# Scores of two heads in one slot, with the low parts of the queries on the two row halves of the array

## The chip, the core and the metric

The kernel runs on one core of one Trainium2 chip. The metric is the time of one execution on the device in microseconds (us); the number shown for a kernel is the median of its runs. TensorE does the matmuls and transposes and writes PSUM, VectorE (DVE) and ScalarE (ACT) do everything elementwise, GpSimd (POOL) little, SyncE (SP) issues most DMAs.

## The reference

Attention over 4 batches of 12 heads, 448 positions, 64 elements per head, then two feed-forward layers over all 1792 tokens, all in float32:

```python
q_n, k_n = rmsnorm(q, g_q), rmsnorm(k, g_k)
scores = (1 / sqrt(64)) * q_n @ k_n.T
attn = exp(scores - max(scores)); attn = attn / (sum(attn) + 1e-9)
x = (attn @ v), heads side by side -> (1792, 768)
x = (sigmoid(x @ w_gate) * (x @ w_val)) @ w_out      # d_ff 1536
out = relu(x @ w_in) ** 2 @ w_out2                   # d_ff 2048
```

## The kernel before

**Sweeps and slots.** The work goes batch by batch. Sweep `s` does both feed-forward layers of batch `s` in 68 steps; a step takes one block of weights and issues its matmuls (18 of 448 columns, line 526 to 528, in most steps; 18 or 24 of 384 columns, line 735 to 737, in the last 16). The attention of batch `s + 1` is laid between these steps: `slots_of` lists its pieces in slots, and after step `i` of the sweep as many slots are run as bring the count to `(i + 1) * total // 66`. A function given to `later(n, ...)` runs `n` steps on, and what is put in `mid` runs when the next step has taken its block. A planner then orders each engine's instructions at build time: it goes by program order as priority, takes an instruction when by its own timeline the inputs are there and the output's tile is free, and takes the next one of lower priority otherwise. Weights are split into high and low parts (`w_split`, lines 177 and 178) three blocks ahead.

**Number formats.** A float32 value is kept as a high part in fp32r, the rounded format that TensorE takes in one pass, and a low part, the rest. A product is then high by high, high by low and low by high. The layers' matmuls do this with three matmuls each.

**Attention of batches 2 and 3** (batches 0 and 1 use other functions, among them `s_mm`, line 275, with plain fp32 operands). Heads go in pairs, with head 0 on partitions 0 to 63 and head 1 on 64 to 127; queries go in four chunks of 112, two chunks (`c2`) at a time.

- `a_hi`, `a_lo`, `a_dma` make the operands of the scores. `ks[:, e]` has for head `e` the high part of the keys on the head's own 64 partitions and the low part on the other 64. `qs[:, e, z]` has the high (`z = 0`) or low (`z = 1`) part of the queries, copied by a DMA to the other 64 partitions too. A matmul over 128 rows so gives the product of a query part with both key parts at once.
- `s_mm2` (line 414): scores of one head and two chunks, four matmuls over 128 rows: both query parts against both key parts. Its tile is one of the pool `att`, which has two tiles of two PSUM banks.
- `s_max2`, `s_exp2`, `s_norm2`: maximum (line 421), exponential (line 433), division by the sum.
- `c_mm2` (lines 455, 456): transposes the weights of attention into an `att` tile; `c_hi` (lines 465, 468) copies the high part out on ScalarE and `c_lo` (lines 473, 477) the low part on VectorE, one step later.
- `pv_mm2` (lines 486, 488): seven matmuls with the values; `pv_half` (line 492) and `pv_add` (line 498) add the two halves of its output.

Slots before take one head each: scores of chunks 0 and 1, transposes of the last head's chunks 2 and 3, scores of chunks 2 and 3, values of the last head, transposes of chunks 0 and 1.

Of the kernel before, what the change touches and what calls it, by code (L numbers as in the profile page):

```python
# [8 lines left out]
F32 = mybir.dt.float32  # L9
# [8 lines left out]
def attention_moe_moe2_kernel(  # L18
# [57 lines left out]
    def att_tile():  # L76
        return att_p.tile([128, 2, 512], F32, tag="att", name="att")
# [325 lines left out]
    def a_dma(st):  # L403
        qs = st["qs"]
        for h in range(2):
            a = slice(h * D, (h + 1) * D)
            z = slice((1 - h) * D, (2 - h) * D)
            nc.sync.dma_start(out=qs[z, h].bitcast(F32), in_=qs[a, h].bitcast(F32))

    def s_mm2(st, e, c2, ps):  # L410
        for i in range(2):
            c = 2 * c2 + i
            for z in range(2):
                nc.tensor.matmul(  # L414
                    out=ps[:QR, i, :S], lhsT=st["qs"][:, e, z, c * QR:(c + 1) * QR], rhs=st["ks"][:, e],
                    start=(z == 0), stop=(z == 1))
        st["s", e, c2] = ps

    def s_max2(st, e, c2):
        nm = sm_p.tile([QR, 2], F32, tag="nm", name="nm")  # L420
        nc.vector.tensor_reduce(out=nm, in_=st["s", e, c2][:QR, :, :S], axis=AX.X, op=ALU.max, negate=True)  # L421
        rq = st["ms"][:, 1].rearrange("p (c h) -> p c h", h=2)[:, 2 * c2:2 * c2 + 2, e]
        with tc.high_priority(offset=200):
            nc.vector.tensor_tensor(out=nm, in0=nm, in1=rq, op=ALU.mult)  # L424
        st["nm", e, c2] = nm
# [23 lines left out]
    def c_mm2(st, e, c2):  # L449
        ps = att_tile().rearrange("p a (k c) -> p (a k) c", k=2)  # L450
        p = st.pop(("p", e, c2))
        for i in range(2):
            for kc in range(NF):
                k0 = i * (S + TAIL) + kc * 128
                nc.tensor.transpose(ps[:, kc, i * QR:(i + 1) * QR], p[:, k0:k0 + 128], ident[:QR, :QR])  # L455
        nc.tensor.transpose(ps[:, NF, 0:QR], p[:, NM:NM + 2 * TAIL], ident[:QR, :QR])
        if c2 == 0:
            parts = one.tile([128, NS, S], F32R, tag="pt", name="parts")
            st["ph", e], st["pl", e] = parts[:, 0:NF + 1], parts[:, NF + 1:NS]
        st["c", e, c2] = ps  # L460

    def c_hi(st, e, c2):
        ps, ph = st["c", e, c2], st["ph", e]
        cs = slice(c2 * QW, (c2 + 1) * QW)
        nc.scalar.copy(out=ph[:, 0:NF, cs], in_=ps[:, 0:NF, 0:QW])
        for i in range(2):
            a, c0 = slice(i * TAIL, (i + 1) * TAIL), c2 * QW + i * QR
            nc.scalar.copy(out=ph[a, NF, c0:c0 + QR], in_=ps[a, NF, 0:QR])

    def c_lo(st, e, c2):  # L470
        ps, ph, pl = st.pop(("c", e, c2)), st["ph", e], st["pl", e]
        cs = slice(c2 * QW, (c2 + 1) * QW)
        nc.vector.tensor_tensor(
            out=pl[:, :, cs], in0=ps[:, 0:NF, 0:QW], in1=ph[:, 0:NF, cs].bitcast(F32), op=ALU.subtract)
        for i in range(2):
            a, c0 = slice(i * TAIL, (i + 1) * TAIL), c2 * QW + i * QR
            nc.vector.tensor_tensor(
                out=ph[(1 - i) * TAIL:(2 - i) * TAIL, NF, c0:c0 + QR], in0=ps[a, NF, 0:QR],
                in1=ph[a, NF, c0:c0 + QR].bitcast(F32), op=ALU.subtract)

    def pv_mm2(st, e):
        o = st["o", e] = att_tile()[:, 0, :S]
        ph, pl = st.pop(("ph", e)), st.pop(("pl", e))
        for kc in range(NF + 1):
            lhsT = st["vs"][:, kc, 2 * e:2 * e + 2].rearrange("p a d -> p (a d)")
            nc.tensor.matmul(out=o, lhsT=lhsT, rhs=ph[:, kc], start=(kc == 0), stop=(kc == NF))  # L486
            if kc < NF:
                nc.tensor.matmul(out=o, lhsT=lhsT, rhs=pl[:, kc], start=False, stop=False)

    def pv_half(st, e):  # L490
        xt = st["xt"] = tmp_p.tile([128, 512], F32, tag="tmp", name="xt")
        nc.scalar.copy(out=xt[e * D:(e + 1) * D, :S], in_=st["o", e][(1 - e) * D:(2 - e) * D])

    def pv_add(st, e):
        a = slice(e * D, (e + 1) * D)
        if e == 0:
            st["o"] = one.tile([128, S], F32, tag="x32", name="x32")
        nc.vector.tensor_tensor(out=st["o"][a], in0=st.pop(("o", e))[a], in1=st.pop("xt")[a, :S], op=ALU.add)

    xtile, xplain = {}, {}  # L500

# [6 lines left out]
    mid = []  # L508

    def later(n, fn, *args):  # L510
        due.setdefault(now[0] + n, []).append((fn, args))
# [241 lines left out]
    def nxt(b, hp):  # L753
        return (b, hp + 1) if hp + 1 < HP else (b + 1, 0)
# [3 lines left out]
    def slots_of(b):  # L758
# [49 lines left out]
            mid.append((a_lo, (st,)))  # L808
            later(1, a_dma, st)

        def do_s2(key, e, c2):
            st = pairs[key]
            s_mm2(st, e, c2, att_tile())
            s_max2(st, e, c2)
            mid.append((s_exp2, (st, e, c2)))
            later(1, s_norm2, st, e, c2)

        def do_c2(key, e, c2):
            st = pairs[key]
            c_mm2(st, e, c2)  # L820
            c_hi(st, e, c2)
            later(1, c_lo, st, e, c2)

        def do_pv2(key, e):
            st = pairs[key]
            pv_mm2(st, e)
            pv_half(st, e)
            later(1, pv_add, st, e)
            if e == 1:
                later(2, x_hi, st)  # L830
                later(2, x_lo, st)
                later(2, lambda: pairs.pop(key))

        def do_stat(key):
            st = pairs[key]
# [5 lines left out]
                later(2, stat_hat, st, 1)  # L841

        if b > 1:
            for h in range(H):
                key, e = (b, h // 2), h % 2
                nk = nxt(*key)
                prev = ((b, (h - 1) // 2), (h - 1) % 2)
                more = nk[0] < B

                def some(fn, nk=nk, more=more):  # L850
                    return [lambda: fn(nk)] if more else []

                add(lambda key=key, e=e: do_s2(key, e, 0), *(some(do_load) if e == 0 else []))
                if h:
                    add(lambda prev=prev: do_c2(*prev, 1))
                add(lambda key=key, e=e: do_s2(key, e, 1))
                if e == 1 and more:
                    add(*some(do_a2))
                if h:
                    add(lambda prev=prev: do_pv2(*prev))  # L860
                if e == 0:
                    add(lambda key=key: do_c2(key, 0, 0), lambda key=key: split_v(pairs[key]), *some(do_stat))
                else:
                    add(lambda key=key: do_c2(key, 1, 0), *some(do_v))
            add(lambda: do_c2((b, HP - 1), 1, 1))
            add(lambda: None)
            add(lambda: do_pv2((b, HP - 1), 1))
            return slots
        if b == 1:
            add(lambda: do_stat((1, 0)))  # L870
# [199 lines left out]
```

## Time and profile before

| what | value |
|---|---|
| median of 3 runs | 1279.74 us (1278.72 to 1280.75) |
| the profiled execution's own time | 1279.0 us |
| its span, first to last instruction | 1277.2 us |
| granted TensorE clock, mean | 0.999 of 2.4 GHz |
| TensorE busy | 1263.8 us, 99% of the span |
| VectorE busy | 941.3 us, 74% |
| ScalarE busy | 798.7 us, 63% |

A busy TensorE is one that has at least one matmul in flight; records of successive matmuls overlap, since they are pipelined, so the spacing from start to start tells what one costs. The chain of work that ended last lies on TensorE for 94% of the span.

### The profile page before, as it was taken

The page shows a single profiled execution, that of the slowest core. Times are in us where ns is not written, and L with a number is a line of the kernel's source. Part 1 is how long each engine was busy: PE and PEld are TensorE (multiplying, and loading weights), DVE is VectorE, ACT ScalarE, POOL GpSimd, SP SyncE. Part 2 cuts the span into 40 slices and gives each one's busy share as a digit, 9 for nine tenths or more (in the row PEclk, how much of TensorE's full clock was granted, in tenths as well). Part 3 has the DMA queues.
Part 4 walks back from the last instruction along what each step waited for, and adds up shares of the span by engine and source line. Part 5 has one row for each costly group of instructions (what it writes and reads, how often), then busy time and mean ns, then how long its engine had stood idle before and what let it go on. Part 6 is the DMA issues. An engine that isn't in the chain of part 4 may idle for free.

```text
span 1277.2 us, 19296 instructions
## 1 busy us (share of the span) xinstructions
PE 1263.8 (99%) x6755; PEld 1111.9 (87%) x6755; DVE 941.3 (74%) x1657; ACT 798.7 (63%) x1582; POOL 154.8 (12%) x152
## 2 busy tenths in 40 slices
PE   8999999999999999999999999999999999999998
PEld 6545888878878999999999999999999999999998
DVE  6857888788974888778876488877897546646964
ACT  5757887667865777656755477765666455524552
POOL 3301422212120001000100000100010001110000
PEclk9999999999999999999999999999999999999999
DMA  5445899897786344344344433433333456663364
GB/s 144 120 133 157 292 333 301 255 298 237 243 289 179 94 111 129 96 119 121 96 104 133 123 106 105 126 102 113 97 92 108 129 183 218 217 220 108 112 185 149
DMA packets 163616, 206.92 MB, mean 162 GB/s; under 512 B 77248, under 2 KB 123840, under 8 KB 163520
## 3 DMA queue, kind: packets, MB, share of 16 engines
q1 hardware_dynamic: 154176, 172.20, 46.6%
q0 software_dynamic: 7488, 33.04, 6.5%
q8 instruction: 53, 0.87, 0.3%
q10 hardware_dynamic: 1856, 0.46, 0.2%
q14 instruction: 43, 0.35, 0.1%
HBM read 161.61 MB, written 38.54 MB: 157 GB/s over the span
## 4 chain that ended last, share of the span: by engine, by line
PE 94%; DVE 2%; ACT 1%; DMA 1%; issue 1%; SPq 1%; POOL 0%; DVEq 0%; ACTq 0%; POOLq 0%
PE acc L526 19%; PE acc L528 19%; PE acc L527 19%; PE acc L737 4%; PE acc L735 4%; PE acc L736 4%; PE att L414 3%; PE att L275 3%; PE att L455 2%; PE acc L329 2%; PE att L486 2%; PE acc L606 2%; PE acc L608 2%; PE acc L607 2%; PE att L329 1%; PE acc L647 1%
## 5 line engine op out<-in xcount | busy, mean ns | idle before, releaser
L526 PE MATMUL acc<-xy,wsp 128*128 128x448 f32 x936 | 345.8, 370 | 2.0 <-ACT wsp L177 1.4
L178 DVE TENSOR_TENSOR wsp<-wraw,wsp 128x768 fp32r<-128x768 f32 x280 | 268.2, 958 | 106.8 <-ACT wsp L177 103.5
L528 PE MATMUL acc<-xy,wsp 128*128 128x448 f32 x936 | 344.5, 368 | 1.5 <-DVE wsp L178 1.5
L527 PE MATMUL acc<-xy,wsp 128*128 128x448 f32 x936 | 344.1, 368 | 0.1
L177 ACT CAST wsp<-wraw 128x768 fp32r<-128x768 f32 x280 | 233.4, 834 | 116.1 <-PE acc L528 38.8
L526 PEld LDWEIGHTS acc<-xy,wsp 128*128 128x128 f32 x936 | 176.3, 188 | 23.4 <-ACT wsp L177 4.3
L528 PEld LDWEIGHTS acc<-xy,wsp 128*128 128x128 f32 x936 | 176.3, 188 | 19.0 <-DVE wsp L178 2.1
L527 PEld LDWEIGHTS acc<-xy,wsp 128*128 128x128 f32 x936 | 176.3, 188 | 15.0 <-issue 0.7
L245 POOL TENSOR_TENSOR ms<-ms,mhalf 112x16 f32<-112x16 f32 (+1 forms) x25 | 84.5, 3381 | 546.8 <-DVE ms L244 456.4
L526 PE MATMUL acc<-hb,wsp 128*128 128x448 f32 x288 | 106.1, 369 | 0.0
L527 PE MATMUL acc<-hb,wsp 128*128 128x448 f32 x288 | 105.8, 367 | 0.0
L528 PE MATMUL acc<-hb,wsp 128*128 128x448 f32 x288 | 105.6, 367 | 0.0
L433 ACT ACTIVATE p<-att,nm,ms 112x448 f32<-112x448 f32 x96 | 68.8, 723 | 45.1 <-DVE nm L424 44.9
L736 PE MATMUL acc<-wsp,rb 128*128 128x384 f32 x288 | 96.9, 337 | 0.0
L737 PE MATMUL acc<-wsp,rb 128*128 128x384 f32 x288 | 96.8, 336 | 0.0
L735 PE MATMUL acc<-wsp,rb 128*128 128x384 f32 x288 | 96.4, 336 | 0.0
L151 ACT ACTIVATE wraw<-raw 128x768 f32<-128x768 f32 x64 | 58.4, 914 | 31.5 <-DVE wsp L178 19.2
L293 ACT ACTIVATE p<-att,nm 112x448 f32<-112x448 f32 x88 | 55.2, 635 | 15.4 <-DVE nm L281 13.8
L421 DVE TENSOR_REDUCE nm<-att 112x2 f32<-112x896 f32 x48 | 52.3, 1089 | 13.0 <-PE att L414 11.9
L159 DVE SCALAR_TENSOR_TENSOR wraw<-wraw,raw 128x768 int32<-128x768 int32 x64 | 61.0, 956 | 0.9
L166 POOL DMA_DIRECT2D w<-wraw x64 | 36.1, 564 | 206.5 <-DVE wraw L159 196.3
L527 PEld LDWEIGHTS acc<-hb,wsp 128*128 128x128 f32 x288 | 54.1, 188 | 5.7 <-DVE wraw L159 0.7
(169 smaller groups left out, 2209.3 us busy)
## 6 DMA issues: line engine op xcount, KB each, us to landing
wraw<-w SPq DMA_DIRECT2D x188, 384.0 KB, 3.1
w<-wraw POOLq DMA_DIRECT2D x64, 384.0 KB, 6.1
raw<-in_moe_w_out_dram SPq DMA_DIRECT2D x28, 768.0 KB, 7.8
raw<-in_moe_w_in_dram SPq DMA_DIRECT2D x16, 768.0 KB, 6.1
raw<-in_moe_w_gate_dram SPq DMA_DIRECT2D x12, 768.0 KB, 6.1
raw<-in_moe_w_val_dram SPq DMA_DIRECT2D x12, 768.0 KB, 6.3
wsrc<-w SPq DMA_DIRECT2D x16, 384.0 KB, 4.3
wt<-wdst POOLq DMA_DIRECT2D x32, 192.0 KB, 2.4
```

Source lines behind the costliest of these rows:

```text
L151: size = nc.scalar.activation(out=t, in_=hi.bitcast(F32), func=AF.Prelu, scale=2.0 ** -112, alpha=2.0 ** 32)
L159: nc.vector.scalar_tensor_tensor(out=ti, in0=ti, scalar=3, in1=hi, op0=ALU.logical_shift_left, op1=ALU.bitwise_or)
L177: nc.scalar.copy(out=sp[:, 0], in_=t)
L178: nc.vector.tensor_tensor(out=sp[:, 1], in0=t, in1=sp[:, 0].bitcast(F32), op=ALU.subtract)
L245: nc.gpsimd.tensor_tensor(out=ms, in0=ms, in1=mhalf[:QR, 0:ms.shape[1]], op=ALU.pow)
L433: nc.scalar.activation(out=p[:, i * (S + TAIL):i * (S + TAIL) + S], in_=ps[:QR, i, :S], func=AF.Exp, bias=nm[:, i:i + 1], scale=rq[:, 2 * ...
L526: nc.tensor.matmul(out=o, lhsT=wh, rhs=xh, start=start, stop=False)
L527: nc.tensor.matmul(out=o, lhsT=wh, rhs=xl, start=False, stop=False)
L528: nc.tensor.matmul(out=o, lhsT=wl, rhs=xh, start=False, stop=stop)
L735: nc.tensor.matmul(out=o, lhsT=rh, rhs=wh, start=(k1 == 0), stop=False)
L736: nc.tensor.matmul(out=o, lhsT=rh, rhs=wl, start=False, stop=False)
L737: nc.tensor.matmul(out=o, lhsT=rl, rhs=wh, start=False, stop=(k1 == K2 - 1))
```

## The change

In batches 2 and 3 a slot now takes both heads of a pair. `s_mm2` gets two tiles, one for each head. It issues the high parts of the queries as before, over 128 rows against both parts of the keys; the low parts of the queries only meet the high parts of the keys, which lie on the head's own 64 partitions, so these matmuls have 64 rows, on the upper half of the array for head 0 and on the lower half for head 1, in alternation. The product of the two low parts falls away. The DMA that copies the queries' parts to the other partitions moves the high part only. Transposes and values of both heads share a slot too, the values' outputs share one tile, and head 1's parts lie in three buffers of the pool `raw64`, the pool of the first sweep's raw weights. The slots of a batch go from 67 (66 in batch 3) to 44, seven for a pair: scores 0, values of the last pair, transposes 0, scores 1, operands of the next pair, transposes 1, and an empty one.

```diff
@@ -405,16 +405,25 @@
         for h in range(2):
             a = slice(h * D, (h + 1) * D)
             z = slice((1 - h) * D, (2 - h) * D)
-            nc.sync.dma_start(out=qs[z, h].bitcast(F32), in_=qs[a, h].bitcast(F32))
-
-    def s_mm2(st, e, c2, ps):
+            nc.sync.dma_start(out=qs[z, h, 0].bitcast(F32), in_=qs[a, h, 0].bitcast(F32))
+
+    def s_mm2(st, c2, tiles):
+        qs, ks = st["qs"], st["ks"]
+        for e in range(2):
+            for i in range(2):
+                c = 2 * c2 + i
+                nc.tensor.matmul(
+                    out=tiles[e][:QR, i, :S], lhsT=qs[:, e, 0, c * QR:(c + 1) * QR], rhs=ks[:, e],
+                    start=True, stop=False)
         for i in range(2):
             c = 2 * c2 + i
-            for z in range(2):
+            for e in range(2):
+                a = slice(e * D, (e + 1) * D)
                 nc.tensor.matmul(
-                    out=ps[:QR, i, :S], lhsT=st["qs"][:, e, z, c * QR:(c + 1) * QR], rhs=st["ks"][:, e],
-                    start=(z == 0), stop=(z == 1))
-        st["s", e, c2] = ps
+                    out=tiles[e][:QR, i, :S], lhsT=qs[a, e, 1, c * QR:(c + 1) * QR], rhs=ks[a, e],
+                    start=False, stop=True)
+        for e in range(2):
+            st["s", e, c2] = tiles[e]
 
     def s_max2(st, e, c2):
         nm = sm_p.tile([QR, 2], F32, tag="nm", name="nm")
@@ -454,48 +463,57 @@
                 k0 = i * (S + TAIL) + kc * 128
                 nc.tensor.transpose(ps[:, kc, i * QR:(i + 1) * QR], p[:, k0:k0 + 128], ident[:QR, :QR])
         nc.tensor.transpose(ps[:, NF, 0:QR], p[:, NM:NM + 2 * TAIL], ident[:QR, :QR])
-        if c2 == 0:
+        if c2 == 0 and e == 0:
             parts = one.tile([128, NS, S], F32R, tag="pt", name="parts")
-            st["ph", e], st["pl", e] = parts[:, 0:NF + 1], parts[:, NF + 1:NS]
+            st["ph", e], st["pt", e], st["pl", e] = parts[:, 0:NF], parts[:, NF], parts[:, NF + 1:NS]
+        elif c2 == 0:
+            st["ph", e], tail, st["pl", e] = (
+                raw_p.tile([128, NF, S], F32R, tag="raw64", name="parts") for _ in range(3))
+            st["pt", e] = tail[:, 0]
         st["c", e, c2] = ps
 
...
-    def pv_mm2(st, e):
-        o = st["o", e] = att_tile()[:, 0, :S]
-        ph, pl = st.pop(("ph", e)), st.pop(("pl", e))
-        for kc in range(NF + 1):
-            lhsT = st["vs"][:, kc, 2 * e:2 * e + 2].rearrange("p a d -> p (a d)")
-            nc.tensor.matmul(out=o, lhsT=lhsT, rhs=ph[:, kc], start=(kc == 0), stop=(kc == NF))
-            if kc < NF:
-                nc.tensor.matmul(out=o, lhsT=lhsT, rhs=pl[:, kc], start=False, stop=False)
+    def pv_mm2(st):
+        o = att_tile()
+        vs = st["vs"]
+        for e in range(2):
+            ph, pt, pl = (st.pop((part, e)) for part in ("ph", "pt", "pl"))
+            for kc in range(NF + 1):
+                lhsT = vs[:, kc, 2 * e:2 * e + 2].rearrange("p a d -> p (a d)")
+                for n, rhs in enumerate((ph[:, kc], pl[:, kc]) if kc < NF else (pt,)):
+                    nc.tensor.matmul(out=o[:, e, :S], lhsT=lhsT, rhs=rhs, start=(kc + n == 0), stop=(kc == NF))
+        for e in range(2):
+            st["o", e] = o[:, e, :S]
 
     def pv_half(st, e):
-        xt = st["xt"] = tmp_p.tile([128, 512], F32, tag="tmp", name="xt")
+        if e == 0:
+            st["xt"] = tmp_p.tile([128, 512], F32, tag="tmp", name="xt")
+        xt = st["xt"]
         nc.scalar.copy(out=xt[e * D:(e + 1) * D, :S], in_=st["o", e][(1 - e) * D:(2 - e) * D])
 
     def pv_add(st, e):
         a = slice(e * D, (e + 1) * D)
         if e == 0:
             st["o"] = one.tile([128, S], F32, tag="x32", name="x32")
-        nc.vector.tensor_tensor(out=st["o"][a], in0=st.pop(("o", e))[a], in1=st.pop("xt")[a, :S], op=ALU.add)
+        nc.vector.tensor_tensor(out=st["o"][a], in0=st.pop(("o", e))[a], in1=st["xt"][a, :S], op=ALU.add)
 
     xtile, xplain = {}, {}
 
@@ -808,28 +826,30 @@
             mid.append((a_lo, (st,)))
             later(1, a_dma, st)
 
-        def do_s2(key, e, c2):
+        def do_s2(key, c2):
             st = pairs[key]
-            s_mm2(st, e, c2, att_tile())
-            s_max2(st, e, c2)
-            mid.append((s_exp2, (st, e, c2)))
-            later(1, s_norm2, st, e, c2)
-
-        def do_c2(key, e, c2):
+            s_mm2(st, c2, [att_tile(), att_tile()])
+            for e in range(2):
+                s_max2(st, e, c2)
+                mid.append((s_exp2, (st, e, c2)))
+                later(1, s_norm2, st, e, c2)
+
+        def do_c2(key, c2):
             st = pairs[key]
-            c_mm2(st, e, c2)
-            c_hi(st, e, c2)
-            later(1, c_lo, st, e, c2)
-
-        def do_pv2(key, e):
+            for e in range(2):
+                c_mm2(st, e, c2)
+                c_hi(st, e, c2)
+                later(1, c_lo, st, e, c2)
+
+        def do_pv2(key):
             st = pairs[key]
-            pv_mm2(st, e)
-            pv_half(st, e)
-            later(1, pv_add, st, e)
-            if e == 1:
-                later(2, x_hi, st)
-                later(2, x_lo, st)
-                later(2, lambda: pairs.pop(key))
+            pv_mm2(st)
+            for e in range(2):
+                pv_half(st, e)
+                later(1, pv_add, st, e)
+            later(2, x_hi, st)
+            later(2, x_lo, st)
+            later(2, lambda: pairs.pop(key))
 
         def do_stat(key):
             st = pairs[key]
@@ -841,30 +861,25 @@
                 later(2, stat_hat, st, 1)
 
         if b > 1:
-            for h in range(H):
-                key, e = (b, h // 2), h % 2
-                nk = nxt(*key)
-                prev = ((b, (h - 1) // 2), (h - 1) % 2)
+            for hp in range(HP):
+                key, nk, prev = (b, hp), nxt(b, hp), (b, hp - 1)
                 more = nk[0] < B
 
                 def some(fn, nk=nk, more=more):
                     return [lambda: fn(nk)] if more else []
 
-                add(lambda key=key, e=e: do_s2(key, e, 0), *(some(do_load) if e == 0 else []))
-                if h:
-                    add(lambda prev=prev: do_c2(*prev, 1))
-                add(lambda key=key, e=e: do_s2(key, e, 1))
-                if e == 1 and more:
-                    add(*some(do_a2))
-                if h:
-                    add(lambda prev=prev: do_pv2(*prev))
-                if e == 0:
-                    add(lambda key=key: do_c2(key, 0, 0), lambda key=key: split_v(pairs[key]), *some(do_stat))
+                add(lambda key=key: do_s2(key, 0), *some(do_load))
+                if hp:
+                    add(lambda prev=prev: do_pv2(prev))
                 else:
-                    add(lambda key=key: do_c2(key, 1, 0), *some(do_v))
-            add(lambda: do_c2((b, HP - 1), 1, 1))
+                    add(lambda: None)
+                add(lambda key=key: do_c2(key, 0), lambda key=key: split_v(pairs[key]), *some(do_stat))
+                add(lambda key=key: do_s2(key, 1))
+                add(*some(do_a2), *some(do_v))
+                add(lambda key=key: do_c2(key, 1))
+                add(lambda: None)
+            add(lambda: do_pv2((b, HP - 1)))
             add(lambda: None)
-            add(lambda: do_pv2((b, HP - 1), 1))
             return slots
         if b == 1:
             add(lambda: do_stat((1, 0)))
```

`c_hi` and `c_lo`, left out above, only name the last column block of the parts (`pt`) separately.

## Rows read from the trace of the kernel before

**Rows 1.** The page: busy us, share and instructions of each engine; TensorE in slices

```profile
PE 1263.8 (99%) x6755; PEld 1111.9 (87%) x6755; DVE 941.3 (74%) x1657; ACT 798.7 (63%) x1582; POOL 154.8 (12%) x152
...
PE   8999999999999999999999999999999999999998
```

**Rows 2.** Stretches: length, busy PE, PEld, DVE, ACT, POOL, clock, DMA share, GB/s

```profile
400.00:700.00 300.00, 300.00 (x1622) 279.26 (x1621) 227.55 (x456) 192.37 (x405) 21.65 (x6) 1.00 0.39 112
700.00:1005.00 305.00, 305.00 (x1651) 284.33 (x1650) 234.53 (x466) 193.15 (x396) 17.63 (x7) 1.00 0.39 111
```

**Rows 3.** Groups by line and shape, 400 to 1005 us: busy, mean ns, idle before

```profile
L421 DVE TENSOR_REDUCE nm<-att 112x2 f32<-112x896 f32 x48 | 52.3, 1089 | 13.0 <-PE att L414 11.9
L414 PE MATMUL att<-ks,qs 128*112 128x448 f32 x192 | 46.9, 366 | 0.0
L473 DVE TENSOR_TENSOR parts<-att,parts 128x672 fp32r<-128x672 f32 x46 | 39.3, 855 | 9.2 <-ACT parts L468 8.7
...
L465 ACT CAST parts<-att 128x672 fp32r<-128x672 f32 x46 | 33.3, 724 | 12.9 <-PE att L456 12.5
...
L477 DVE TENSOR_TENSOR parts<-att,parts 64x112 fp32r<-64x112 f32 x92 | 25.0, 272 | 1.3
L468 ACT CAST parts<-att 64x112 fp32r<-64x112 f32 x92 | 22.8, 248 | 0.5
```

**Rows 4.** Timeline of TensorE, batch 2: start, length, what (successive records of one line merged)

```profile
414.21 0.37 PE L528 MATMUL acc<-xy,wsp 128*128 128x448 f32 x1
414.42 0.98 PE L414 MATMUL att<-ks,qs 128*112 128x448 f32 x4
415.23 0.37 PE L526 MATMUL acc<-xy,wsp 128*128 128x448 f32 x1
```

**Rows 5.** Timeline of TensorE around a group of half-row matmuls, batch 1

```profile
377.09 0.33 PE L735 MATMUL acc<-wsp,rb 128*128 128x384 f32 x1
...
379.17 0.34 PE L735 MATMUL acc<-wsp,rb 128*128 128x384 f32 x1
379.44 1.01 PE L275 MATMUL att<-kq 64*112 64x448 f32 x4
380.38 0.44 PE L736 MATMUL acc<-wsp,rb 128*128 128x384 f32 x1
380.66 0.34 PE L737 MATMUL acc<-wsp,rb 128*128 128x384 f32 x1
```

**Rows 6.** The same group's two pairs, timeline in windows of 0.02 us

```profile
379.44 0.63 PE L275 MATMUL att<-kq 64*112 64x448 f32 x2
...
379.91 0.54 PE L275 MATMUL att<-kq 64*112 64x448 f32 x2
```

**Rows 7.** Timeline of TensorE, a group of eight half-row matmuls

```profile
353.65 1.76 PE L275 MATMUL att<-kq 64*112 64x448 f32 x8
355.34 0.44 PE L737 MATMUL acc<-wsp,rb 128*128 128x384 f32 x1
```

**Rows 8.** Groups by line and shape, whole span: plain fp32 over 128 rows

```profile
L647 PE MATMUL acc<-xplain,wsp 128*128 128x448 f32 x48 | 18.6, 543 | 0.0
```

**Rows 9.** Timeline of TensorE, batch 1's score slot for chunks 2 and 3

```profile
283.55 0.83 PE L311 MATMUL att<-ident,p 112*128 112x112 f32 x7
284.32 1.01 PE L275 MATMUL att<-kq 64*112 64x448 f32 x4
285.26 0.47 PE L528 MATMUL acc<-xy,wsp 128*128 128x448 f32 x1
...
289.10 1.01 PE L275 MATMUL att<-kq 64*112 64x448 f32 x4
```

**Rows 10.** Timeline of TensorE, the first scores of batch 3

```profile
726.83 1.18 PE L414 MATMUL att<-ks,qs 128*112 128x448 f32 x5
...
735.16 0.77 PE L414 MATMUL att<-ks,qs 128*112 128x448 f32 x3
```

**Rows 11.** Timelines of TensorE and VectorE, one head's transposes and their subtractions

```profile
524.32 0.26 PE L456 MATMUL att<-ident,p 112*128 112x112 f32 x1
...
527.42 0.56 DVE L477 TENSOR_TENSOR parts<-att,parts 64x112 fp32r<-64x112 f32 x2
```

More of the change, by code (lines that the diff above doesn't have):

```diff
@@ L456, in c_mm2 @@
         nc.tensor.transpose(ps[:, NF, 0:QR], p[:, NM:NM + 2 * TAIL], ident[:QR, :QR])
-        if c2 == 0:
+        if c2 == 0 and e == 0:
             parts = one.tile([128, NS, S], F32R, tag="pt", name="parts")
-            st["ph", e], st["pl", e] = parts[:, 0:NF + 1], parts[:, NF + 1:NS]
+            st["ph", e], st["pt", e], st["pl", e] = parts[:, 0:NF], parts[:, NF], parts[:, NF + 1:NS]
[3 more added lines that the diff above has]
+            st["pt", e] = tail[:, 0]
         st["c", e, c2] = ps
     def c_hi(st, e, c2):
-        ps, ph = st["c", e, c2], st["ph", e]
+        ps, ph, pt = st["c", e, c2], st["ph", e], st["pt", e]
         cs = slice(c2 * QW, (c2 + 1) * QW)
-        nc.scalar.copy(out=ph[:, 0:NF, cs], in_=ps[:, 0:NF, 0:QW])
+        nc.scalar.copy(out=ph[:, :, cs], in_=ps[:, 0:NF, 0:QW])
         for i in range(2):
             a, c0 = slice(i * TAIL, (i + 1) * TAIL), c2 * QW + i * QR
-            nc.scalar.copy(out=ph[a, NF, c0:c0 + QR], in_=ps[a, NF, 0:QR])
+            nc.scalar.copy(out=pt[a, c0:c0 + QR], in_=ps[a, NF, 0:QR])
     def c_lo(st, e, c2):
-        ps, ph, pl = st.pop(("c", e, c2)), st["ph", e], st["pl", e]
+        ps, ph, pt, pl = st.pop(("c", e, c2)), st["ph", e], st["pt", e], st["pl", e]
         cs = slice(c2 * QW, (c2 + 1) * QW)
         nc.vector.tensor_tensor(
-            out=pl[:, :, cs], in0=ps[:, 0:NF, 0:QW], in1=ph[:, 0:NF, cs].bitcast(F32), op=ALU.subtract)
+            out=pl[:, :, cs], in0=ps[:, 0:NF, 0:QW], in1=ph[:, :, cs].bitcast(F32), op=ALU.subtract)
         for i in range(2):
@@ L477, in c_lo @@
             nc.vector.tensor_tensor(
-                out=ph[(1 - i) * TAIL:(2 - i) * TAIL, NF, c0:c0 + QR], in0=ps[a, NF, 0:QR],
-                in1=ph[a, NF, c0:c0 + QR].bitcast(F32), op=ALU.subtract)
-    def pv_mm2(st, e):
-        o = st["o", e] = att_tile()[:, 0, :S]
-        ph, pl = st.pop(("ph", e)), st.pop(("pl", e))
-        for kc in range(NF + 1):
-            lhsT = st["vs"][:, kc, 2 * e:2 * e + 2].rearrange("p a d -> p (a d)")
-            nc.tensor.matmul(out=o, lhsT=lhsT, rhs=ph[:, kc], start=(kc == 0), stop=(kc == NF))
-            if kc < NF:
-                nc.tensor.matmul(out=o, lhsT=lhsT, rhs=pl[:, kc], start=False, stop=False)
+                out=pt[(1 - i) * TAIL:(2 - i) * TAIL, c0:c0 + QR], in0=ps[a, NF, 0:QR],
+                in1=pt[a, c0:c0 + QR].bitcast(F32), op=ALU.subtract)
+    def pv_mm2(st):
[9 more added lines that the diff above has]
+            st["o", e] = o[:, e, :S]
     def pv_half(st, e):
-        xt = st["xt"] = tmp_p.tile([128, 512], F32, tag="tmp", name="xt")
+        if e == 0:
+            st["xt"] = tmp_p.tile([128, 512], F32, tag="tmp", name="xt")
+        xt = st["xt"]
         nc.scalar.copy(out=xt[e * D:(e + 1) * D, :S], in_=st["o", e][(1 - e) * D:(2 - e) * D])
```

## The prediction

> **What bounds the kernel now.** I read four views. First the page's busy times and its forty slices: TensorE is busy in nine tenths or more of all slices but the first and the last [rows 1]. Then the stretches: batch 2's attention runs beside the layers of batch 1 from about 400 to 700 us, batch 3's beside those of batch 2 from 700 to 1005 us, and in both TensorE is busy for the whole stretch, 300.00 of 300 us and 305.00 of 305 us, while VectorE has a quarter of its time free and ScalarE a third [rows 2]. So in the two stretches which the change touches, nothing makes TensorE wait: a TensorE instruction saved there is time saved one for one, and a TensorE delay added there is time lost one for one. Work moved on the other engines counts only where it makes TensorE wait, which it doesn't now. Third, the groups of lines in these stretches, for what attention costs each engine [rows 3]. Fourth, the timeline of TensorE around single groups of score matmuls, for the spacing from start to start, which is what counts on a pipelined engine: the busy time of one record (366 ns for a score matmul) overlaps with the next one.
>
> **What the scores cost before.** A call of `s_mm2` issues four matmuls over all 128 rows. From its first start at 414.42 to the next matmul's start at 415.23 is 0.81 us, so 0.2025 us each; the switch from a layer's matmul (128 columns of weights) to these (112 columns) costs nothing that the starts show [rows 4]. There are 192 of them in the two batches [rows 3], so scores hold TensorE for 192 x 0.2025 = 38.9 us. Per pair of heads and pair of query chunks (24 such cases: 2 batches, 6 pairs, 2 halves) that is 8 x 0.2025 = 1.62 us.
>
> **What they would cost after.** The new `s_mm2` issues for the same case four matmuls over 128 rows (high parts of the queries against both parts of the keys) and four over 64 rows, two on the upper and two on the lower half, in alternation. If the halves overlap fully, that is 4 + 2 spacings instead of 8, a saving of 2 x 0.2025 = 0.405 us, over 24 cases 9.7 us. Nothing in the two stretches has such half matmuls now, but batches 0 and 1 do: `s_mm`, line 275, with 64 rows each, in plain fp32. They show two things.
>
> They do overlap: the first two records of a group span 0.63 us together, which is the length of one of them, so they start together, and the second two again [rows 6]. A group of eight takes 355.34 - 353.65 = 1.69 us to the next start [rows 7], one of four 380.38 - 379.44 = 0.94 us [rows 5]; the two further pairs cost 0.75 us, 0.375 us a pair. A full fp32 record of the same 448 columns costs 18.6/48 = 0.39 us [rows 8], so a pair costs no more than one full matmul.
>
> But going to half rows and back is not free. Before the group the layer's matmuls start every (379.17 - 377.09)/12 = 0.173 us. From the last of these, at 379.17, to the second one behind the group, at 380.66, is 1.49 us [rows 5]. Two ordinary spacings are 0.35 us, two pairs 0.75 us; what is left, 0.39 us, is the price of the two changes, into half rows and out. It lies about evenly: the first half matmul starts 0.27 us after the last full one instead of 0.17 and runs 0.09 us longer than the later ones (0.63 against 0.54), and the full one behind the group shows the same (0.44 against 0.33).
>
> The Trainium skill has this as a rule: in "TensorEngine Tiling (Array Packing)", section Tiling Modes, it states that a change of the tiling mode drains TensorE. The trace agrees, with 0.39 us for the way in and out; the rule gives no price. The sum is the same with or without it.
>
> So a case costs 6 x 0.2025 + 0.39 = 1.61 us instead of 1.62: the gain of the pairs and the price of the switch cancel, 24 x 0.015 = 0.4 us saved. For the fp32r halves the price is bounded below by nothing (the layers' matmuls go from 128 to 112 columns for nothing, [rows 4]) and above by the 0.39 us of line 275; I take the latter, since that is the same change of rows, and the pieces of it look like an emptied pipeline, not like something of fp32.
>
> **Splitting.** The two heads' scores now lie in two tiles of a pool that has two. A half matmul overlaps its partner only if they are next to each other in TensorE's order, and the planner puts an instruction in as soon as its tile is free and goes on with other work otherwise. Where two tiles are asked for in one slot today, it shows this: batch 1's slot for chunks 2 and 3 runs the first tile's scores at 284.32 and the second's at 289.10, with some 18 layer matmuls between them, since the second tile was still being emptied after the transposes at 283.55 [rows 9]; line 414 itself has a group of five and one of three [rows 10].
>
> In the new order the second score slot of a pair (`do_s2(key, 1)`) follows `do_c2(key, 0)` directly. Now 44 slots share 66 steps, so the next slot is alternately one and two layer steps away, and a pair has seven slots: in pairs 0, 2 and 4 of a batch the distance is one step, 18 x 0.2025 = 3.6 us, in the others two. A tile comes free when `c_lo` is done with it. For one head that is 3.7 us after its last transpose starts (524.32 to 527.42 + 0.56) [rows 11]. For two heads in one slot the second one's copies (0.72 + 2 x 0.25) and subtractions (0.86 + 2 x 0.27) stand behind the first one's [rows 3]: about 1.4 us more, some 5 us, against 3.6 us. So with one step between, the first head's tile is free in time and the second's mostly not. Then the first head does two full and two half matmuls alone, and the second the same later: 8 x 0.2025 + 2 x 0.39 = 2.40 us, 0.78 us more than before. Six cases of 24 are exposed; VectorE's load decides each, and I count three split: 3 x 0.78 = 2.3 us. All other score slots have two or three steps.
>
> **What costs nothing.** Transposes, value matmuls, maxima, exponentials, copies and subtractions keep number and size; they only come in bursts of two heads. Their cover is that VectorE and ScalarE run at three quarters and two thirds of the stretches [rows 2] and the layers' weights are split three blocks ahead; if a burst made a layer wait, one maximum (1.09 us [rows 3]) is what it would typically wait for. `pv_mm2` of both heads takes one tile instead of two. The values' parts of head 1 move into buffers of the weight pool which only batch 0's layers and the last ones use. `a_dma` moves half the bytes on SP's queue; the scores that read them come several slots later. The last `do_pv2` is now one step earlier than before, which can't hurt the next layers.
>
> **Sum.** Own time of the profiled execution 1279.0 us (span 1277.2): 1279.0 - 0.4 + 2.3 = 1280.9. The runs' median is 0.7 us above that execution, so 1281.6 us. What a measurement can tell from no change is about 0.2%, 2.6 us: 1277.2 to 1282.3.
>
> **The rivals.**
>
> Slower, by split pairs: if the planner splits six to twelve cases instead of three (all one-step cases, and the others when VectorE is late), the price is 5 to 9 us, 1284 to 1289. It decides from four split cases on. For it speaks how regularly batch 1's second tile comes late; against it that most cases have two or three steps.
>
> Slower, by halves that don't overlap: line 275 is plain fp32, the new halves are fp32r. If these run one after the other, a case costs 8 x 0.2025 + 0.39, 24 x 0.39 = 9.4 us, 1289. Nothing in the trace says that the type matters; the pairs of line 275 start together.
>
> Faster: the switch is cheaper for fp32r to fp32r. At half its price the cases save 24 x 0.21 = 5.0 us, less 3 x 0.6 for split ones: 1276.5; at no price 9.7 us: 1270. The Trainium skill's "TensorE: Matmul & The Clock Gate", section Part 3: Packing small matmuls, has it this way: concurrent tiles cost one matmul and about 4 ns per further tile, with no word of a switch. The records of line 275 agree as to the start together, but not as to the sum, since 0.39 us remain.
>
> No splits at all: 1279.3, no change.
>
> **How the numbers follow.** Forecast, two to four splits: 0.45, of which 0.36 inside the 0.2% and 0.09 above. No split: 0.12. More splits or a new wait: 0.26. No overlap: 0.06. Cheaper switch: 0.11. So faster 0.11, same 0.48, slower 0.41. The range leaves out the halves that don't overlap (0.06), the free switch (0.06) and the upper end of the splits (0.06): 1276.5 to 1287. The likeliest case alone: 1280.5 to 1282.5.
>
> **What would show it.** After: 96 full and 96 half matmuls in place of line 414's 192; halves in pairs that start together, 0.2 us from pair to pair; about 0.1 us lost at the first half matmul's start, 0.09 us more in its length, and the same at the first full one behind it. Split cases appear as groups of four lone records (two full, two half) some microseconds apart. TensorE busy for the whole stretch as before. I am wrong if the switch shows no such gaps (then it is faster), if more than five cases are split, if halves start 0.2 us apart, or if TensorE shows idle time with a cause on VectorE or ScalarE between 400 and 1005 us.

## The result and the profile after

| | median (runs) | ratio to before, 95% interval |
|---|---|---|
| before | 1279.23 us (1278.45 to 1280.75, 4) | |
| after | 1291.61 us (1290.94 to 1294.66, 4) | 1.0100 (1.0081 to 1.0119) |

The change costs 12.4 us, one per cent; 1281.6 us was forecast and 1287 us was the upper end of the range. The profiled execution took 1291.91 us, its span is 1289.9 us, 12.7 us more than before.

The page of the changed kernel, the lines that answer to [rows 1]:

```profile
PE 1276.1 (99%) x6755; PEld 1103.2 (86%) x6755; DVE 939.8 (73%) x1657; ACT 800.6 (62%) x1582; POOL 157.4 (12%) x152
...
PE   8999999999999999999999999999999999999998
```

Its two stretches, with the columns of [rows 2]:

```profile
400.00:700.00 300.00, 300.00 (x1590) 269.25 (x1589) 224.66 (x453) 190.58 (x402) 19.96 (x6) 1.00 0.36 106
700.00:1005.00 305.00, 305.00 (x1614) 273.78 (x1613) 228.00 (x451) 189.52 (x385) 21.29 (x7) 1.00 0.36 104
```

TensorE still never rests in them, so no new wait appeared. It gets less done instead: 1590 matmuls in the first stretch where [rows 2] have 1622. The loss is in what TensorE's instructions cost, as the prediction said it would have to be. The groups of the new lines, whole span (columns of [rows 3]), have as many full and half matmuls as foreseen:

```profile
L422 PE MATMUL att<-ks,qs 64*112 64x448 f32 x96 | 28.8, 410 | 0.0
L415 PE MATMUL att<-ks,qs 128*112 128x448 f32 x96 | 26.5, 366 | 0.0
```

Two timelines of TensorE show what they cost. First a visit with both heads together (start, length, what):

```profile
417.82 0.37 PE L546 MATMUL acc<-xy,wsp 128*128 128x448 f32 x1
418.02 0.98 PE L415 MATMUL att<-ks,qs 128*112 128x448 f32 x4
418.93 0.66 PE L422 MATMUL att<-ks,qs 64*112 64x448 f32 x4
419.52 0.47 PE L544 MATMUL acc<-xy,wsp 128*128 128x448 f32 x1
419.83 0.36 PE L545 MATMUL acc<-xy,wsp 128*128 128x448 f32 x1
```

From the first start to the next layer matmul is 419.52 - 418.02 = 1.50 us, and that one takes 0.31 us to its successor instead of about 0.20: 1.61 us in all, where before two visits took 1.62 us. That the halves run together is seen in the same timeline, window of 0.02 us from 418.92 on:

```profile
418.93 0.46 PE L422 MATMUL att<-ks,qs 64*112 64x448 f32 x2
```

Both halves of the first pair have started within the window, like the two of [rows 6]. Then a case that fell apart:

```profile
439.83 0.56 PE L415 MATMUL att<-ks,qs 128*112 128x448 f32 x2
440.32 0.66 PE L422 MATMUL att<-ks,qs 64*112 64x448 f32 x2
440.92 0.47 PE L546 MATMUL acc<-xy,wsp 128*128 128x448 f32 x1
441.23 0.36 PE L544 MATMUL acc<-xy,wsp 128*128 128x448 f32 x1
...
442.66 0.57 PE L415 MATMUL att<-ks,qs 128*112 128x448 f32 x2
443.16 0.66 PE L422 MATMUL att<-ks,qs 64*112 64x448 f32 x2
443.75 0.47 PE L545 MATMUL acc<-xy,wsp 128*128 128x448 f32 x1
444.06 0.36 PE L546 MATMUL acc<-xy,wsp 128*128 128x448 f32 x1
```

Two full matmuls and two halves of one head, eight layer matmuls, then the other head's. The halves of one head use the same row half, so they have no partner: these two take 440.92 - 440.32 = 0.60 us, as long as the four halves above (419.52 - 418.93 = 0.59 us). So a partner costs nothing, but a pair takes 0.3 us from its start to the next one, where the prediction's sign named 0.2; the excess is part of the 0.39 us that it counted for the switch. One such visit is 440.92 - 439.83 = 1.09 us plus 0.11 us in the matmul behind it, 1.20 us; two are 2.40 us. Counted over the trace, the scores come in 44 visits (a visit is an unbroken row of score matmuls): four whole cases, 38 visits of one head, and the first case of batch 3 in a group of five matmuls and one of three, as [rows 10] has it before the change too. **19 of the 24 cases were cut between the heads**; I had counted three.

Summed from start to start, the score matmuls took 39.1 us before (the prediction had 38.9) and take 49.3 us after, and the 44 matmuls behind a visit lose 0.107 us each, 4.7 us: together (49.26 - 39.14) + 4.7 = 14.8 us. Against it, the layers' other matmuls take some 3.2 us less than before, and the kernel's first matmuls, which the change doesn't touch, took 1.1 us longer: 14.8 - 3.2 + 1.1 = 12.7 us, the difference of the spans. The 3.2 us have two sources. About 1.7 us are a difference of pace (last section). About 1.6 us have nothing to do with the change: in the profiled execution of before the granted TensorE clock was 0.50 (1.2 GHz) for a while in batch 0's layers, right behind a wait of 0.86 us for weights, and in that of after it stayed at 1.00 (2.4 GHz). Ten matmuls run in the first row (before), 17 in the second (after, about the same place; columns of [rows 2]):

```profile
145.10:148.51 3.41, 3.41 (x10) 3.02 (x11) 2.99 (x5) 2.60 (x6) 3.41 (x2) 0.50 0.54 181
146.00:149.40 3.40, 3.40 (x17) 3.12 (x18) 3.40 (x5) 3.40 (x6) 3.40 (x1) 1.00 0.49 161
```

### The profile page after: what moved, and what is told of

Read it like the earlier page. It is cut to its first block, busy times and chain, and to the rows that moved or that the text cites. A ratio compares the mean times of both kernels' runs of the same rounds, so it can differ in the third digit from the quotient of the medians.

```text
span 1289.9 us, 19302 instructions
## 1 busy us (share of the span) xinstructions
PE 1276.1 (99%) x6755; PEld 1103.2 (86%) x6755; DVE 939.8 (73%) x1657; ACT 800.6 (62%) x1582; POOL 157.4 (12%) x152
## 4 chain that ended last, share of the span: by engine, by line
PE 94%; DVE 2%; ACT 1%; issue 1%; DMA 1%; SPq 1%; POOL 0%; DVEq 0%; ACTq 0%; POOLq 0%
PE acc L544 19%; PE acc L546 19%; PE acc L545 19%; PE acc L753 4%; PE acc L754 4%; PE acc L755 4%; PE att L275 3%; PE att L502 3%; PE att L464 2%; PE att L422 2%; PE acc L329 2%; PE acc L625 2%; PE att L415 2%; PE acc L626 2%; PE acc L624 2%; PE att L329 1%
## 5 line engine op out<-in xcount | busy, mean ns | idle before, releaser
L430 DVE TENSOR_REDUCE nm<-att 112x2 f32<-112x896 f32 x48 | 52.0, 1089 | 18.2 <-PE att L422 17.7
```

## The experiments

Kernels that were compared share a chip and the runs of the kernel before; each has the median of before beside it. The halves without the product of the two low parts are also in those below that keep halves (e2, e3, e4, e7, e8); e1, e5 and e6 compute the full product as before does.

**e1: the new slots without halves.** The changed kernel, but the low parts over all 128 rows, and the DMA of both query parts:

```diff
-            nc.sync.dma_start(out=qs[z, h, 0].bitcast(F32), in_=qs[a, h, 0].bitcast(F32))
+            nc.sync.dma_start(out=qs[z, h].bitcast(F32), in_=qs[a, h].bitcast(F32))
...
-                    out=tiles[e][:QR, i, :S], lhsT=qs[a, e, 1, c * QR:(c + 1) * QR], rhs=ks[a, e],
+                    out=tiles[e][:QR, i, :S], lhsT=qs[:, e, 1, c * QR:(c + 1) * QR], rhs=ks[:, e],
```

> The changed kernel with its two-head slots and tiles as they are, but the low parts of the queries multiplied over all 128 rows as before the change (and copied by the DMA again), so that no matmul has half rows. Theory of the split visits (the loss is 19 of 24 score visits that were cut in two, 0.76 us each, because a lone visit pays the way into half rows and out and finds no partner): without half rows a cut costs nothing, so about 1279 us, 1278 to 1281. Rival, two-head slots (bursts of two heads' work on VectorE and ScalarE, and the tile pool, make TensorE late): they are all still there, so about 1291 us.

Measured: 1277.55 us (1275.44 to 1283.49, 10 runs) against 1280.58; ratio 0.9985 (0.9967 to 1.0003), no clear difference. In its trace 38 visits still hold one head each, so the cases fall apart here too, and it costs nothing. So neither two heads in a slot nor the cutting by itself is the loss. It takes the half rows to make a cut dear.

**e2: half rows without a partner.** The kernel before with its slots of one head; only the low parts use the head's own 64 rows:

```diff
-        for i in range(2):
-            c = 2 * c2 + i
-            for z in range(2):
+        a = slice(e * D, (e + 1) * D)
+        for z in range(2):
+            for i in range(2):
+                c = 2 * c2 + i
+                rows = slice(0, 128) if z == 0 else a
...
-                    out=ps[:QR, i, :S], lhsT=st["qs"][:, e, z, c * QR:(c + 1) * QR], rhs=st["ks"][:, e],
+                    out=ps[:QR, i, :S], lhsT=st["qs"][rows, e, z, c * QR:(c + 1) * QR], rhs=st["ks"][rows, e],
```

> The kernel before, with its slots of one head, but the low parts of the queries against the high parts of the keys alone, on the head's own 64 rows; a visit is two full and two half matmuls, and no half has a partner. Theory of the split visits: all 48 visits are lone ones, 48 x 0.39 = 18.7 us more than before, 1298 us, less up to 3 us for layer matmuls that run at the faster of the two spacings seen (0.203 and 0.207 us): 1295 to 1298. Rival, two-head slots: there are none here, so 1279 to 1281.

Measured: 1298.76 us (1296.42 to 1300.46, 4 runs) against 1280.58; ratio 1.0147 (1.0125 to 1.0169). That is 0.8 us above the expected range. 18.2 us for 48 visits is 0.38 us a visit. The timeline of one:

```profile
417.80 1.16 PE L416 MATMUL att<-ks,qs 128*112 128x448 f32 x4
418.89 0.47 PE L528 MATMUL acc<-xy,wsp 128*128 128x448 f32 x1
419.20 0.36 PE L529 MATMUL acc<-xy,wsp 128*128 128x448 f32 x1
```

(The profile merges two full and two half matmuls of one line.) 418.89 - 417.80 = 1.09 us and 0.11 us behind it, against 0.81 us in [rows 4]: 0.39 us. The price of going to half rows and back that the prediction took from line 275's plain fp32 [rows 5] holds for fp32r.

**e3: a partner that can't come late.** A tile holds both heads of one chunk instead of both chunks of one head, so a pair of halves writes one tile and needs only that:

```diff
-                    out=tiles[e][:QR, i, :S], lhsT=qs[a, e, 1, c * QR:(c + 1) * QR], rhs=ks[a, e],
+                    out=tiles[i][:QR, e, :S], lhsT=qs[a, e, 1, c * QR:(c + 1) * QR], rhs=ks[a, e],
...
-        st["nm", e, c2] = nm
+        st["nm", i, c2] = nm
```

(`s_max2` and `s_exp2` go by chunk in the same way.)

> The changed kernel with the scores laid out so that a tile holds both heads of one chunk, not both chunks of one head: each tile gets two full matmuls and one pair of halves, and the pair can no longer be cut apart. Theory of the split visits: a whole visit costs 1.60 us as before the change, two separate ones 2 x (3 x 0.2025 + 0.39) = 2.00 us, 0.38 more than before. With some 19 of 24 separate: 1279 + 7 = 1286 us, less up to 3 us for the layers' spacing: 1283 to 1286. Rival, two-head slots: 1291. Rival, half rows cost more than the 0.39 us a visit: above 1288.

Measured: 1284.68 us (1283.26 to 1290.11, 8 runs) against 1280.58; ratio 1.0038 (1.0021 to 1.0056). Every half has its partner now; the timeline of two chunks of a pair in a row:

```profile
416.25 0.57 PE L415 MATMUL att<-ks,qs 128*112 128x448 f32 x2
416.75 0.45 PE L420 MATMUL att<-ks,qs 64*112 64x448 f32 x2
417.14 0.66 PE L415 MATMUL att<-ks,qs 128*112 128x448 f32 x2
417.73 0.45 PE L420 MATMUL att<-ks,qs 64*112 64x448 f32 x2
418.11 0.47 PE L541 MATMUL acc<-xy,wsp 128*128 128x448 f32 x1
```

The switch is now paid for each chunk, 48 times where whole cases would pay it 24 times: 48 x (0.39 - 0.2025) = 9.0 us more than before by this sum, 8.6 us in the trace, less some 2.3 us by the layers' faster pace (last section). So of the 12.4 us some 8 us go when the halves are never alone, but a switch for every pair still costs more than the pair saves.

**e4: the halves held until both heads are there.** The changed kernel, the halves ordered behind the second head's last full matmul:

```diff
-                nc.tensor.matmul(
+                full = nc.tensor.matmul(
...
+        with tc.issue_after(full.ins):
```

> The changed kernel, with the four half matmuls of a visit queued behind the last full matmul of the second head, by an edge of order on TensorE alone; full matmuls may still come early. Theory of the split visits: all 24 visits have whole pairs, 24 x (1.60 - 1.62), so 1279 us, less up to 3 us for the layers' spacing: 1276 to 1280. The first head's scores are finished later, which costs nothing while TensorE has layer matmuls to do. Rival, two-head slots: 1291, or worse, since the first head's tile is held longer. Rival, half rows cost more than 0.39 us a visit: above 1282.

Measured: 1304.00 us (1300.56 to 1307.50, 4 runs) against 1280.58; ratio 1.0189 (1.0160 to 1.0218). My expectation missed by 2%; of its rivals, the tile held longer is the one that came. The halves did come in fours in 23 of the 24 cases, and the scores' own cost is back to that of before: 46.5 us from start to start with two waits of 4.8 us in it, so 36.9 us, and 2.5 us in the matmuls behind, against 39.1. But TensorE now waits. Its page has (columns of [rows 1])

```profile
PE 1268.8 (98%) x6755; PEld 1104.3 (85%) x6755; DVE 938.7 (72%) x1657; ACT 798.3 (61%) x1582; POOL 163.9 (13%) x152
```

in a span of 1300.0 us, 31.2 us not busy against 13.8 us after. Its list of TensorE's waits (us in total, times, longest) and the timeline of all engines around one:

```profile
PE att L503 <- ACT p L443: 10.7, 4, 4.7
PE acc L545 <- ACT rl L727: 2.1, 2, 1.1
PE att L465 <- DVE x L517: 1.9, 1, 1.9
```

```profile
625.80 0.57 PE L415 MATMUL att<-ks,qs 128*112 128x448 f32 x2
...
626.30 0.66 PE L423 MATMUL att<-ks,qs 64*112 64x448 f32 x4
626.86 0.96 DVE L178 TENSOR_TENSOR wsp<-wraw,wsp 128x768 fp32r<-128x768 f32 x1 [2.46 <-ACT wsp L177]
627.85 2.09 DVE L431 TENSOR_REDUCE nm<-att 112x2 f32<-112x896 f32 x2
...
630.13 0.72 ACT L443 ACTIVATE p<-att,nm,ms 112x448 f32<-112x448 f32 x1 [3.30 <-DVE nm L434]
...
631.70 2.83 PE L503 MATMUL att<-parts,vs 128*128 128x448 f32 x7 [4.74 <-ACT p L443]
```

The values (line 503) stand directly behind the halves in TensorE's order and need one of the two `att` tiles. VectorE first finishes a split of weights (626.86), and both tiles are held by the scores until the maxima (627.85 to 629.94) and the first head's exponentials are done, and nothing else was placed between. Early halves let the first head's maximum run while the second head waits for its tile; held ones make both begin together.

Behind this wait the granted clock fell as well, to 0.50 (1.2 GHz; columns of [rows 2]):

```profile
631.90:635.31 3.41, 3.41 (x10) 3.02 (x10) 2.38 (x9) 1.16 (x4) 0.00 (x0) 0.50 0.00 0
918.62:922.03 3.41, 3.41 (x18) 3.12 (x18) 3.32 (x8) 2.55 (x6) 3.37 (x1) 1.00 0.00 0
```

Ten matmuls ran in the first row and 18 in the second, of the same length at clock 1.00. The profile has three such stretches, at 631.9, 915.2 and 959.6 us, each behind waits on the tiles (4.74 us; 0.90 and 1.87 us; 4.73 us); at half the clock each loses about 1.7 us, an estimate from its length. No run of e4, nor of e8 below, has a mean granted clock above 0.996, while runs of before reach 1.000.

**e5: the kernel before with 128 columns of weights.** Set up on the observation that the layers' matmuls have two paces, and that the slower one follows the scores (last section). The scores' weights are widened from 112 to 128 columns; the 16 further rows of the output are read by nobody:

```diff
-        qs = st["qs"] = one.tile([128, 2, 2, S], F32R, tag="qs", name="qs")
+        qf = st["qf"] = one.tile([128, 4 * S + 16], F32R, tag="qs", name="qs")
+        nc.gpsimd.memset(qf[:, 4 * S:].bitcast(F32), 0.0)
+        qs = st["qs"] = qf[:, 0:4 * S].rearrange("p (e z s) -> p e z s", e=2, z=2)
...
+                c0 = (2 * e + z) * S + c * QR
...
-                    out=ps[:QR, i, :S], lhsT=st["qs"][:, e, z, c * QR:(c + 1) * QR], rhs=st["ks"][:, e],
+                    out=ps[:, i, :S], lhsT=st["qf"][:, c0:c0 + 128], rhs=st["ks"][:, e],
```

> The kernel before, with one edit: the scores' weights have 128 columns instead of 112 (the next chunk's 16 columns, or 16 zeros behind the last, give 16 output rows that nobody reads). Seen so far: a layer's 448-column matmuls start every 0.2026 us or every 0.2066 us in long stretches; in the kernel before, 1034 of 3672 run in the slower way; of the stretches behind a score visit that began in the faster way 23 of 34 went on in the slower one, behind transposes nearly all are fast, and the value matmuls, with 128 columns, changed nothing in 16 of 16. Theory of the spacing (112-column weights of a full-row matmul knock the stream into the slower spacing): score visits no longer change it, fewer than 300 slow matmuls, 3 to 5 us saved: 1274 to 1277 beside about 1279.5 of before. Rival (any interruption does it by chance): about 1000 slow, 1279 to 1280.

Measured: 1275.21 us (1272.56 to 1280.17, 12 runs) against 1280.12; ratio 0.9966 (0.9952 to 0.9981). It is faster than before by 0.34%, and so than the changed kernel too.

**e6: e1 and e5 together.** Two heads in a slot, full rows, 128 columns.

> The two-head slots of the changed kernel with full-row low parts, as in the run with full rows, and with 128-column weights in the scores. Theory of the spacing: two-head slots alone were 0.998 of before with 724 slow matmuls; with under 300 slow ones 1274 to 1277 us. Rival, any interruption: 1277 to 1279.

Measured: 1276.26 us (1272.96 to 1280.85, 12 runs) against 1280.12; ratio 0.9966 (0.9950 to 0.9981). The small gain of e1, which is not clear of noise, doesn't add to that of e5. That fits one source for both, the slow stretches of the layers' matmuls (last section): 957 matmuls are at the slow pace before, 716 in e1, none in e5 and none here.

**e7: more distance between the slots.** The changed kernel with three empty slots more in each pair, so that both scores and both transposes are about two steps behind the last slot that takes tiles (the values and the next pair's operands stay one step behind the scores):

```diff
+                add(lambda: None)
                 add(lambda key=key: do_c2(key, 0), lambda key=key: split_v(pairs[key]), *some(do_stat))
+                add(lambda: None)
                 add(lambda key=key: do_s2(key, 1))
                 add(*some(do_a2), *some(do_v))
+                add(lambda: None)
                 add(lambda key=key: do_c2(key, 1))
```

> The changed kernel with its half-row pairs, and three empty slots more for each pair of heads (before the first transposes, before the second scores, before the second transposes), so that 62 slots share the 66 steps and each piece has about two steps after the one whose tiles it needs. Reading of the prediction, that a visit is cut where the slot ahead is only one step away: at most four cut visits, 1277 to 1281 us. Rival: with two tiles for scores, operands, transposes and values in turn, the second head's tile is always some microseconds later than the first's and each slot passes the lag on: 15 or more cut, 1287 to 1292 us.

Measured: 1291.82 us (1291.08 to 1295.76, 6 runs) against 1280.12; ratio 1.0097 (1.0079 to 1.0116), as the changed kernel itself. Again 38 visits hold one head, 19 cases. My reading, that one step of distance decides, fell. Its timelines of TensorE and of VectorE show a case with more than two steps between transposes and scores and still cut:

```profile
429.46 0.74 PE L464 MATMUL att<-ident,p 112*128 112x112 f32 x6
...
430.14 0.74 PE L464 MATMUL att<-ident,p 112*128 112x112 f32 x6
...
438.52 0.56 PE L415 MATMUL att<-ks,qs 128*112 128x448 f32 x2
...
441.35 0.57 PE L415 MATMUL att<-ks,qs 128*112 128x448 f32 x2
```

```profile
434.21 0.56 DVE L490 TENSOR_TENSOR parts<-att,parts 64x112 fp32r<-64x112 f32 x2
...
436.93 0.56 DVE L490 TENSOR_TENSOR parts<-att,parts 64x112 fp32r<-64x112 f32 x2
```

Line 490 is the last reader of each head's tile. The second head's comes 436.93 - 434.21 = 2.72 us after the first's, and the second head's scores 441.35 - 438.52 = 2.83 us after the first's. On the chip both tiles were free at 437.49, before either score started, but the order had been fixed at build time.

**e8: e4 and e7 together**, to see whether distance takes e4's waits away.

> The changed kernel with the half matmuls held behind the second head's full ones and with the three further empty slots for each pair. Theory: whole visits cost what the old ones did, 24 x (1.60 - 1.62), and the price of the hold alone was TensorE waiting for tiles that the first head's scores kept longer, some 20 us. If room between the slots takes these waits away: 24 whole visits, 1277 to 1280 us. Rival, the attention of a pair goes round two tiles and no empty slot makes that shorter: the waits stay, above 1290 us with whole pairs. Either way the whole visits' own price stays at 1.6 us.

Measured: 1299.05 us (1298.26 to 1301.18, 4 runs) against 1279.03; ratio 1.0159 (1.0126 to 1.0192). 23 of 24 cases whole, and the waits are still there, as in its list of TensorE's waits:

```profile
PE att L503 <- ACT p L443: 10.5, 4, 4.7
```

So they don't hang on the distance of the slots, and holding the halves isn't the way to keep them together in this order.

## Why the prediction was wrong

**What held.** TensorE bounds both stretches, and no wait of VectorE or ScalarE appeared in them (300.00 and 305.00 us busy). Two heads in a slot cost nothing (e1). The halves overlap: they start together in pairs, and "halves that don't overlap" is out. The switch costs 0.39 us for fp32r as for fp32 (e2: 0.38 us a visit over 48 visits), so the "cheaper switch" is out as well. A whole case costs 1.61 us, as forecast, and a split one 2.40 us, as forecast. The Trainium skill's "TensorEngine Tiling (Array Packing)", section Tiling Modes, has TensorE drain at a change of mode; e2's 0.39 us a visit fits that. The Trainium skill's "TensorE: Matmul & The Clock Gate", section Part 3: Packing small matmuls, has tiles of different rows overlap, and the common start of a pair agrees; it names no price for the switch, and e2's switches cost 18.2 us.

**The step that failed** is in the part on splitting: "Six cases of 24 are exposed; VectorE's load decides each, and I count three split: 3 x 0.78 = 2.3 us. All other score slots have two or three steps." The price per case was right, the count was not: 19 x 0.78 = 14.8 us instead of 2.3. All six cases that I had called exposed were cut, and so were 13 that I had called safe: ten of the scores of chunks 0 and 1, and three of chunks 2 and 3 with two steps between. It is the "slower, by split pairs" rival, which I stopped at twelve cases and 1289 us. With 19 the same sum gives 1279.7 - 0.4 + 14.8 = 1294.1 us. The layers' pace, which I didn't foresee, takes about 1.7 us off, and the stretch at half clock, which the profile of before has and that of after hasn't, about 1.6 us; the kernel's first matmuls put 1.1 us on: 1291.9, against 1291.61 measured. None of the three was foreseen, and that they made the miss smaller is luck.

**Why so many.** I asked whether the second tile is free by the time the scores' slot comes, and took distance in steps as the answer. e7 shows that distance is not what decides, since with the scores and transposes spread the same number falls apart. What the rows show is that the two tiles don't come free together. Two heads in a slot means that the second head's copies and subtractions follow the first's, 2.7 us later in e7's rows above. The operands of the next pair and the values also take one of the two tiles between the heads' turns: in the changed kernel's trace the transposes of two heads of one slot start at 451.91 and 460.49, and the next pair's scores, which need the same two tiles, at 462.20 and 468.56. An order that takes each matmul as soon as its tile is free then issues the first head's four matmuls at once, halves included, whatever the distance. This last step is argued, not shown: that the planner's own timeline has the tiles free at such different moments is taken from the resemblance of the two differences (2.72 and 2.83 us), and its timeline is not in the trace. Shown are the cuts, their price (e1, e2), and that more distance doesn't mend them (e7). [rows 9] showed the pattern, 4.8 us between two tiles of one slot, and I took it as a sign of too little distance, not of separate release.

**What stays open.** Why no layer matmuls stand between e4's halves and its values, where 5 us of them would hide the wait, was not settled. Nor was a version with more than two tiles tried, which would test the account above.

## What to carry to other kernels

Packing two half matmuls saves one matmul for each pair, and each excursion into half rows costs about two (0.39 us here), so count how many pairs stand in one excursion: two pairs break even, one loses, and a half without a partner loses all of it. No run here has more than two such fp32r pairs in one excursion. Partners that write separately released buffers were pulled apart here in 19 of 24 cases, by an order that issues as soon as a buffer is free; count on most cases being cut, not only on those where the distance is short, or give both one buffer (e3), and then count the switches anew. A hold that forces them together moves the wait to the next user of those buffers (e4), and behind the longest of these waits the granted clock fell.

## What the runs showed of the hardware that I had not expected

The layers' matmuls of 448 columns have two paces at the same granted clock of 1.00. The timeline of TensorE in the kernel before, first and last of 37 starts behind a visit of line 414 (same weights, same shapes):

```profile
418.88 0.97 PE L414 MATMUL att<-ks,qs 128*112 128x448 f32 x4
...
419.90 0.37 PE L527 MATMUL acc<-xy,wsp 128*128 128x448 f32 x1
...
427.33 0.37 PE L527 MATMUL acc<-xy,wsp 128*128 128x448 f32 x1
```

and in e5 the same stretch, again 37 starts:

```profile
419.04 0.97 PE L417 MATMUL att<-ks,qs 128*128 128x448 f32 x4
...
420.05 0.36 PE L530 MATMUL acc<-xy,wsp 128*128 128x448 f32 x1
...
427.33 0.37 PE L530 MATMUL acc<-xy,wsp 128*128 128x448 f32 x1
```

(427.33 - 419.90)/36 = 0.2064 us against (427.33 - 420.05)/36 = 0.2022 us. Counted over the traces, in uninterrupted rows of at least five such matmuls, without each row's first spacing and without rows that a wait or the half clock stretches, and with a mean spacing on either side of 0.2048 us: 957 matmuls of the kernel before are at the slow pace, 557 after, 413 in e3 (the counts in the expectations took in some more). In the kernel before, 23 of 34 visits of the scores that came in at the fast pace left it slow, and the transposes put all 25 slow rows between 400 and 1005 us back to fast; with weights of 128 columns (e5) none of 35 visits left it slow. In the changed kernel 10 of 11 visits that came in slow left fast. So the weights' 112 columns, or the 112 output rows that go with them, set off the slow pace, at least in this place; by what mechanism, the runs don't show. The prediction read from [rows 4] that the step to 112 columns costs nothing: that holds for the visit, not for the row behind it. The slow rows that went, 957 - 557 = 400 matmuls at some 0.0042 us, are the 1.7 us by which the changed kernel lost less than its cuts cost. All of them, 957 x 0.0042 = 4.0 us, are nearly the 4.3 us (0.34%) that e5 gains with nothing but wider weights.
